# Attention feeding a rational feed-forward layer: q and k loaded as 512-byte rows, and their transposes done head by head as quarter-array products with the identity

## The chip, the cores and the metric

The kernel runs on one core of a Trainium2 chip. The time is device microseconds of that core. The kernel before took 615.79 us, the median of three runs (615.35 to 616.71); the execution that was profiled took 618.84 us.

## The reference, cut to what matters

Two stages follow each other: causal attention over 4 batches, 12 heads, 448 tokens and 64 numbers a head, and a feed-forward layer with a rational activation on the result, laid out as 1792 tokens by 768.

```python
# q, k, v: (4, 12, 448, 64) float32
scores = scale * np.matmul(q, k.transpose(0, 1, 3, 2))
scores = np.where(mask, -1000000000.0, scores)          # causal
scores = scores - np.max(scores, axis=-1, keepdims=True)
attn = np.exp(scores)
attn = attn / (np.sum(attn, axis=-1, keepdims=True) + 1e-09)
attn_out = np.matmul(attn, v)
x = attn_out.transpose(0, 2, 1, 3).reshape(1792, 768)
h = x @ w_in                                            # 768 -> 2048
P = a[0] + a[1] * h + a[2] * h**2 + a[3] * h**3
Q = 1.0 + abs(b[0]) * abs(h) + abs(b[1]) * h**2
out = (P / (Q + 1e-6)) @ w_out                          # 2048 -> 768
```

The weights come as 64-bit floats; the kernel turns them into 32-bit ones itself, beside the attention.

## The kernel before

Attention is done for 24 pairs of heads, one pair after the other in a loop over `p`. A pair fills the 128 rows of the matrix engine's array: head 0 in the lower 64, head 1 in the upper 64. The order of the work is written out by hand in the tables `HEAD`, `FIRST` and `ORDER`; every entry is a step and, behind an @, how many pairs it lags. All engines take the steps of one loop turn in the table's order. So in one turn the matrix engine (PE) does, in this order:

- `c` (line 365, tile psC): 32 transposes of the normalised exponentials of the pair before, each on a 64-row half of the array;
- `qk` (line 279, tile psA): the transposes of q and k of the *next* pair. The loaded tile holds 112 tokens on partitions, four blocks of tokens, both heads side by side, so one transpose takes 64 tokens (or the remaining 48) by 128 numbers, both heads at once. That is 2 tensors x 4 blocks x 2 (64 and 48 tokens, index `x`) = 16 transposes;
- `s` (line 311, tile psS): the scores of the pair, 7 query blocks of 64 rows against 64 to 448 keys, for each of the two heads. Every product sits on one quarter of the array: rows by head, columns by `half((1 + b + j) % 2)`. 14 products, which the trace shows as 28 matmuls, since a 32-bit product runs in two passes (a transpose runs in one);
- `d` (line 389, tile psD): exponentials times v of two pairs ago, 8 products on half the array's columns, 16 matmuls in the trace.

The other engines work beside it. VectorE (DVE) takes the masked maximum of each score block (line 322), copies half of psC (377) and converts weights (168, 174). ScalarE (ACT) does the exponentials with their sums (332), the other half of psC (375), the copy of psA into `QK` (294) and the results of psD (409). GpSimd (POOL) normalises the exponentials (346) and converts weights (158, 162). PSUM banks go round in two rings, so a matmul waits until ACT or DVE has read the bank's last content.

All transfers are issued by the SyncE queue (SP) in program order: q and k of the pair four turns ahead (line 247, four transfers of 112 KB), v of this pair (lines 253 and 256, three transfers), every second turn a 768 KB load of weights (143 or 148) and a 384 KB store (180). Every transfer waits for the landing of the one that stands eight places ahead of it, since eight completion semaphores are used in turn. v has three buffers, q and k four each. After the attention (about 145 us) the two matrix products of the feed-forward layer follow until the end.

Of the kernel before, what the change touches and what calls it, by code (L numbers as in the profile page):

```python
# [8 lines left out]
F32 = mybir.dt.float32  # L9
# [47 lines left out]
def kernel(  # L57
# [11 lines left out]
    nc = tc.nc  # L69
    B, H, S, D = q.shape  # L70
    DM, DFF = moe_w_in.shape
    P = 128
    CP = 112
    NB = S // CP
# [21 lines left out]
    ident = const.tile([P, P], F32, name="ident")  # L96
# [138 lines left out]
    raw, QK, AT, pv, SUM, REC, psa, pss, psr, psc, nmx = {}, {}, {}, {}, {}, {}, {}, {}, {}, {}, {}  # L235
# [3 lines left out]
    def stage_load(p):  # L239
        if p in raw:  # L240
            return
        b, hp = divmod(p, HP)
        raw[p] = {}
        for n, src in (("q", q), ("k", k)):
            t = raw[p][n] = ld.tile([CP, NB, 2, D], F32, tag=n, bufs=4, name=f"{n}raw")
            for j in range(2):
                nc.sync.dma_start(out=t[:, :, j], in_=src[b, 2 * hp + j].rearrange("(c p) d -> p c d", p=CP))

    def stage_load_v(p):
        b, hp = divmod(p, HP)  # L250
# [10 lines left out]
    def half(j):  # L261
        return slice(j * D, (j + 1) * D)
# [3 lines left out]
    def ring(x, name):  # L266
        if x:
            return ps_t.tile([P, 512], F32, tag="y", bufs=3, name=name)
        n = banks.pop(0)
        banks.append(n)  # L270
        return (ps_s if n == 3 else ps_t).tile([P, 512], F32, tag=f"x{n}", name=name)

    def qk_pe(p):
        ps = psa[p] = [ring(x, "psA") for x in range(2)]
        for n, src in enumerate(("q", "k")):
            for c in range(NB):
                for x, w in enumerate((QB, CP - QB)):
                    r, lo = slice(x * QB, x * QB + w), (n * NB + c) * w
                    nc.tensor.transpose(  # L279
                        ps[x][:, lo:lo + w], raw[p][src][r, c].rearrange("p j d -> p (j d)"), ident[r, r]  # L280
                    )
        if p == 0:
            keep_warm(4)

    def qk_ev(p, x):
        if p not in QK:
            QK[p] = qk.tile([P, 2, S], F32, tag="qk", name="qkt")
        lo, hi = x * QB, (QB, CP)[x]
        o = QK[p].rearrange("p n (c r) -> p (n c) r", r=CP)[:, :, lo:hi]
        i = psa[p][x][:, :2 * NB * (hi - lo)].rearrange("p (c r) -> p c r", r=hi - lo)  # L290
        if p < 2 and x == 1:
            nc.vector.tensor_copy(out=o, in_=i)
        else:
            nc.scalar.copy(out=o, in_=i)
# [132 lines left out]
    def conv(p, part):  # L427
# [17 lines left out]

    tasks = {
        "ld": stage_load, "lv": stage_load_v,
        "qk": qk_pe, "qx": lambda p: qk_ev(p, 0), "qy": lambda p: qk_ev(p, 1),
        "s": stage_b_pe, "m": stage_b_max, "e": stage_b_exp, "sm": stage_b_sum, "r": stage_b_rec, "n": stage_b_norm,
        "c": c_pe, "a": lambda p, h: c_ev(p, h, 0), "v": lambda p, h: c_ev(p, h, 1),  # L450
# [410 lines left out]
    with tc.manual_schedule():  # L861
# [13 lines left out]
        ld = es_r.enter_context(pool(name="ld", bufs=2, side="right"))  # L875
# [4 lines left out]
        for x in range(2):  # L880
            m = mask[half(x), S - QB:]
            nc.gpsimd.affine_select(
                out=m, in_=m, compare_op=ALU.is_ge, fill=-1e9 / SCALE, base=0, pattern=[[-1, QB]], channel_multiplier=1,
# [24 lines left out]
        def keep_warm(n):  # L908
            for _ in range(n):
                nc.tensor.matmul(idle, warm, warm, start=True, stop=True, skip_group_check=True)  # L910
# [89 lines left out]
        for j in range(HF):  # L1000
            n = j + 5
# [44 lines left out]
```

## Time and profile before

| what | us |
|---|---|
| median of three runs | 615.79 (615.35 to 616.71) |
| profiled execution | 618.84 |
| its span in the trace | 617.1 |
| PE busy in the span | 597.3 (97%) |
| DVE / ACT / POOL busy | 536.2 / 449.8 / 171.8 |

The span runs from the first to the last instruction of the program; 1.7 us of the profiled execution lie outside it. Busy time of PE counts a matmul from its start to its modelled end, and matmuls overlap in the pipeline, so the start times of successive groups tell more than the busy share. The trace is read by stage: the attention up to about 145 us, and the feed-forward layer after it. PE's granted clock is 1.00 (2.4 GHz) throughout.

### The profile page before, as it was taken

The numbers are of one execution on the slowest core, as the hardware profiler recorded it, in microseconds if no ns is written. First come the engines' busy times: TensorE is split into PE (matmuls) and PEld (weight loads), VectorE is DVE, ScalarE is ACT, GpSimd is POOL, SyncE is SP. The second block draws the span as 40 slices with busy tenths as digits, with TensorE's granted clock in tenths as the row PEclk, the third lists the DMA queues.
The fourth block names the chain that finished last, engine by engine and source line by source line (L and its number), as shares of the span: only waits on it lengthen the run. The fifth ranks groups of instructions, "written<-read, shape, count | busy, mean of one in ns | idle before, by whom it ended". The sixth has DMA issues, their size and how long they took to land.

```text
span 617.1 us, 12747 instructions
## 1 busy us (share of the span) xinstructions
PE 597.3 (97%) x4656; PEld 497.7 (81%) x4656; DVE 536.2 (87%) x1034; ACT 449.8 (73%) x920; POOL 171.8 (28%) x251
## 2 busy tenths in 40 slices
PE   7999999889999999999999999989999999999997
PEld 5666666557788888888888888878999999997886
DVE  4899999976689999999998888888999999986950
ACT  5999999986776867778877567566576776777721
POOL 3788888785544311112333100000000000000000
PEclk9999999999999999999999999999999999999999
DMA  8978697888468988889985663333263344148774
GB/s 163 239 176 213 171 217 206 204 201 276 145 264 286 332 311 304 304 304 313 353 303 197 216 240 106 141 128 129 102 216 122 126 153 149 57 157 319 236 237 177
DMA packets 105727, 131.00 MB, mean 212 GB/s; under 512 B 70592, under 2 KB 83008, under 8 KB 105664
## 3 DMA queue, kind: packets, MB, share of 16 engines
q1 hardware_dynamic: 105664, 130.18, 66.4%
q8 instruction: 37, 0.61, 0.4%
q14 instruction: 26, 0.21, 0.1%
HBM read 99.49 MB, written 30.67 MB: 211 GB/s over the span
## 4 chain that ended last, share of the span: by engine, by line
PE 69%; DVE 15%; ACT 7%; issue 4%; DMA 3%; POOL 2%; SPq 0%; ACTq 0%; DVEq 0%; POOLq 0%
PE psO L597 19%; PE psH L227 16%; PE psQ L699 12%; PE psM L593 10%; PE psD L389 4%; PE psS L311 4%; PE psC L365 3%; ACT e L332 2%; DVE psS L322 2%; DMA vraw<-in_v_dram 1%; DVE u L168 1%; PE psA L279 1%; DVE at L377 1%; POOL e L346 1%; DVE p L754 1%
## 5 line engine op out<-in xcount | busy, mean ns | idle before, releaser
L597 PE MATMUL psO<-whl,gh 128*128 128x512 f32 x448 | 160.0, 393 | 1.3 <-DMA whl<-whl 1.1
L227 PE MATMUL psH<-xs,whl 128*128 128x512 f32 x576 | 136.8, 391 | 0.5 <-DVE p L493 0.4
L593 PE MATMUL psM<-whl,gh 128*128 128x256 f32 x448 | 126.0, 282 | 0.0
L227 PEld LDWEIGHTS psH<-xs,whl 128*128 128x128 f32 x576 | 105.9, 188 | 22.6 <-DVE p L493 0.7
L597 PEld LDWEIGHTS psO<-whl,gh 128*128 128x128 f32 x448 | 84.0, 188 | 21.1 <-ACT kept L762 1.4
L346 POOL TENSOR_SCALAR e<-e,r 128x192 f32<-128x192 f32 (+6 forms) x168 | 80.0, 499 | 35.6 <-DVE r L342 18.6
L593 PEld LDWEIGHTS psM<-whl,gh 128*128 128x128 f32 x448 | 84.5, 189 | 1.3
L699 PE MATMUL psQ<-xpart,wq 128*128 128x384 f32 x432 | 78.5, 336 | 4.3 <-ACT xpart L615 1.7
L332 ACT ACTIVATE e<-psS,nm 128x448 f32<-128x448 f32 (+6 forms) x168 | 78.0, 506 | 6.0 <-DVE nm L322 5.7
L597 PE MATMUL psO<-whl,gl 128*128 128x512 f32 x224 | 81.2, 391 | 0.1
L699 PEld LDWEIGHTS psQ<-xpart,wq 128*128 128x128 f32 x432 | 74.8, 188 | 5.8 <-ACT xpart L615 2.0
L322 DVE CUSTOM_DVE_ANT_0 psS<-psS,mask 128x64 f32<-128x64 f32 (+6 forms) x168 | 65.3, 455 | 1.8 <-PE psS L311 1.7
L593 PE MATMUL psM<-whl,gl 128*128 128x256 f32 x224 | 63.1, 282 | 0.0
L389 PE MATMUL psD<-at,vraw 128*64 128x448 f32 (+3 forms) x384 | 47.6, 386 | 4.9 <-DMA vraw<-in_v_dram 2.5
L500 ACT ACTIVATE w<-w 128x512 f32<-128x512 f32 x32 | 20.2, 632 | 42.0 <-DVE w L485 42.0
L158 POOL TENSOR_SCALAR u<-raw 128x768 f32<-128x768 f32 x32 | 35.3, 1103 | 55.0 <-DMA raw<-in_moe_w_out_dram 23.4
L389 PEld LDWEIGHTS psD<-at,vraw 128*64 128x64 f32 x384 | 27.0, 136 | 29.0 <-issue 12.0
L597 PEld LDWEIGHTS psO<-whl,gl 128*128 128x128 f32 x224 | 42.0, 188 | 9.3 <-DVE gl L790 0.4
L311 PE MATMUL psS<-qkt 64*64 64x192 f32 (+6 forms) x672 | 48.1, 391 | 1.2 <-ACT e L332 0.9
L593 PEld LDWEIGHTS psM<-whl,gl 128*128 128x128 f32 x224 | 42.3, 189 | 0.0
L377 DVE COPY at<-psC 128x512 f32<-128x512 f32 x48 | 32.5, 680 | 8.6 <-PE psC L365 8.5
L332 ACT ACTIVATION_READ_ACCUMULATOR e<-psS,nm 128x1 f32 x168 | 39.6, 237 | 0.0
(110 smaller groups left out, 1101.9 us busy)
## 6 DMA issues: line engine op xcount, KB each, us to landing
whl<-whl SPq DMA_DIRECT2D x64, 768.0 KB, 4.4
w<-w SPq DMA_DIRECT2D x54, 384.0 KB, 5.0
raw<-in_moe_w_in_dram SPq DMA_DIRECT2D x16, 768.0 KB, 5.7
raw<-in_moe_w_out_dram SPq DMA_DIRECT2D x16, 768.0 KB, 5.6
w<-u SPq DMA_DIRECT2D x29, 384.0 KB, 3.1
qraw<-in_q_dram SPq DMA_DIRECT2D x48, 112.0 KB, 3.6
kraw<-in_k_dram SPq DMA_DIRECT2D x48, 112.0 KB, 3.6
out_dram<-osb SPq DMA_DIRECT2D x13, 384.0 KB, 3.3
```

The lines of the kernel that those rows point to most:

```text
L158: nc.gpsimd.tensor_scalar(out=u.bitcast(F32), in0=y, scalar1=0.0, scalar2=1.0, op0=ALU.mult, op1=ALU.mult)
L227: nc.tensor.matmul(ps, w[:, c * P:(c + 1) * P], xs[ck, part, c // K3][:, c % K3], start=(c == 0 and n == 0), stop=(c == KD - 1 and n == 2),)
L311: nc.tensor.matmul(pss[p, b][half((1 + b + j) % 2)], QK[p][half(j), 0, b * QB:(b + 1) * QB], QK[p][half(j), 1, :b_w[b]], start=True, stop= ...
L322: nc.vector.tensor_tensor_reduce(out=s, in0=s, in1=mask[:, S - w:], scale=-SCALE, scalar=3e38, op0=ALU.add, op1=ALU.min, accum_out=nmx[p][ ...
L332: nc.scalar.activation(out=E[p % 2][i][:, :w], in_=pss[p, i], func=AF.Exp, bias=nmx[p][:, i:i + 1], scale=-1.0, accum_out=SUM[p % 2][:, i, ...
L346: nc.gpsimd.tensor_scalar(out=e, in0=e, scalar1=REC[p][:, i:i + 1], scalar2=0.0, op0=ALU.mult, op1=ALU.add)
L377: nc.vector.tensor_copy(out=o, in_=i)
L389: nc.tensor.matmul(ps[half(j), lo * QB:S], v[:, j, c], a[h][:, slot * QB:(slot + 7 - lo) * QB], start=(c == 0), stop=(c == 3), skip_group_ ...
L500: nc.scalar.activation(out=w, in_=w, func=AF.Abs)
L593: nc.tensor.matmul(acc["m", k], g, w[:, 512:], start=first and (k % 2 == 0 or each), stop=last, skip_group_check=True)
L597: nc.tensor.matmul(acc[k], g, w[:, :512], start=first, stop=last)
L699: nc.tensor.matmul(q_bank[j, bank], w[:, wp_, c * P:(c + 1) * P], xp_[:, c], start=(first and n == 0), stop=(n == 3 * K3 - 1), skip_group_ ...
```

## The change

One pair's q is now one transfer, and its k another, instead of two each. A partition `p` gets, of each half `g` of a head's tokens, the two neighbouring tokens 2p and 2p+1, which lie next to each other in memory: runs of 512 bytes in place of 256. The tile holds the heads as an outer index, so the two heads of a token are no longer side by side, and one transpose can't take both. Each is done by itself, as an ordinary 32-bit product with the identity, on the quarter of the array given by `x` (rows) and the head `j` (columns). The copy out of PSUM puts the tokens back in order with a step of two in its writes.

```diff
-            t = raw[p][n] = ld.tile([CP, NB, 2, D], F32, tag=n, bufs=4, name=f"{n}raw")
-            for j in range(2):
-                nc.sync.dma_start(out=t[:, :, j], in_=src[b, 2 * hp + j].rearrange("(c p) d -> p c d", p=CP))
+            t = raw[p][n] = ld.tile([CP, 2, 2, 2, D], F32, tag=n, bufs=4, name=f"{n}raw")
+            nc.sync.dma_start(
+                out=t.rearrange("p j g c d -> p (j g) (c d)"),
+                in_=src[b, 2 * hp:2 * hp + 2].rearrange("j (g p c) d -> p (j g) (c d)", g=2, c=2),
+            )
...
-                    nc.tensor.transpose(
-                        ps[x][:, lo:lo + w], raw[p][src][r, c].rearrange("p j d -> p (j d)"), ident[r, r]
-                    )
+                    for j in range(2):
+                        nc.tensor.matmul(
+                            ps[x][half(j), lo:lo + w], raw[p][src][r, j, c // 2, c % 2], ident[r, r],
+                            start=True, stop=True, skip_group_check=True,
+                        )
...
-        o = QK[p].rearrange("p n (c r) -> p (n c) r", r=CP)[:, :, lo:hi]
-        i = psa[p][x][:, :2 * NB * (hi - lo)].rearrange("p (c r) -> p c r", r=hi - lo)
+        o = QK[p].rearrange("p n (g r c) -> p (n g) c r", g=2, c=2)[:, :, :, lo:hi]
+        i = psa[p][x][:, :2 * NB * (hi - lo)].rearrange("p (g c r) -> p g c r", c=2, r=hi - lo)
```

On PE, one turn of the loop stood like this around the transposes (psA's two tiles are its two banks, for 64 and 48 tokens; a size is rows out by columns moved):

```order
L365 MATMUL psC_954<-ident_69,e06_184 128x64
L279 MATMUL psA_979<-ident_69,qraw_601 128x64 [waits DMAHW6_49,DMAHW5_49,Activation_49]
L279 MATMUL psA_980<-ident_69,qraw_601 128x48 [waits PE_49]
...
L279 MATMUL psA_979<-ident_69,kraw_604 128x64 [waits DMAHW7_49,DMAHW0_49]
L279 MATMUL psA_980<-ident_69,kraw_604 128x48
...
L311 MATMUL psS_1008<-qkt_885 64x320 [waits Activation_49]
```

With the change the same place reads (one row is one product, x2 two alike; lines moved by three or four):

```order
L369 MATMUL psC_1338<-ident_69,e06_184 128x64
L282 MATMUL psA_1363<-ident_69,qraw_957 64x64 [waits DMAHW1_49,Activation_49]
L282 MATMUL psA_1363<-ident_69,qraw_957 64x64
L282 MATMUL psA_1364<-ident_69,qraw_957 64x48 [waits PE_49]
...
L282 MATMUL psA_1363<-ident_69,kraw_959 64x64 [waits DMAHW2_49]
L282 MATMUL psA_1364<-ident_69,kraw_959 64x48 x2
...
L315 MATMUL psS_1406<-qkt_1271 64x320 [waits Activation_49]
```

Nothing moved past anything: between psC and psS stand 32 products of 64 output rows in place of 16 transposes of 128, and q and k each wait for one transfer instead of two.

On SP, the transfers of one turn that loads weights (raw) were:

```order
L247 DMA qraw<-in_q_dram 112x4x64 [waits DMAHW3_49]
L247 DMA qraw<-in_q_dram 112x4x64 [waits DMAHW4_49]
L247 DMA kraw<-in_k_dram 112x4x64 [waits DMAHW5_49]
L247 DMA kraw<-in_k_dram 112x4x64 [waits DMAHW6_49]
L148 DMA raw_869<-in_moe_w_out_dram 128x1536 [waits DMAHW7_49,DVE_49]
L253 DMA vraw_175<-in_v_dram 128x3x64 [waits DMAHW0_49,PE_49]
L253 DMA vraw_175<-in_v_dram 128x3x64 [waits DMAHW1_49,PE_49]
L256 DMA vraw_175<-in_v_dram 64x2x64 [waits DMAHW2_49,PE_49]
```

and are now:

```order
L246 DMA qraw<-in_q_dram 112x4x128 [waits DMAHW1_49]
L246 DMA kraw<-in_k_dram 112x4x128 [waits DMAHW2_49]
L148 DMA raw_961<-in_moe_w_out_dram 128x1536 [waits DMAHW3_49,DVE_49]
L255 DMA vraw_175<-in_v_dram 128x3x64 [waits DMAHW4_49,PE_49]
L255 DMA vraw_175<-in_v_dram 128x3x64 [waits DMAHW5_49,PE_49]
L258 DMA vraw_175<-in_v_dram 64x2x64 [waits DMAHW6_49,PE_49]
```

Two transfers fewer stand ahead of the weights and of v, and eight semaphores now span more bytes. ACT, DVE and POOL keep their instructions and their order.

## Rows read from the trace of the kernel before

**Rows 1.** Busy time by stage; columns: stretch, length, each engine's busy time, PEclk, DMA.

```profile
0.00:21.00 21.00, 17.12 (x220) 12.14 (x220) 11.49 (x53) 14.30 (x48) 8.83 (x34) 1.00 0.89 189
21.00:37.30 16.30, 16.30 (x280) 11.29 (x276) 15.52 (x58) 16.26 (x57) 13.41 (x24) 1.00 0.84 203
37.30:94.00 56.70, 56.45 (x924) 37.59 (x920) 56.70 (x209) 55.49 (x199) 47.99 (x81) 1.00 0.82 202
94.00:145.30 51.30, 45.85 (x756) 31.57 (x752) 44.48 (x164) 44.86 (x161) 39.86 (x66) 1.00 0.83 217
145.30:617.00 471.70, 461.57 (x2488) 405.06 (x2488) 408.02 (x553) 318.90 (x463) 61.70 (x49) 1.00 0.62 214
```

**Rows 2.** Timeline of PE, one undisturbed turn; columns: start us, us, engine, line, what.

```profile
21.00 1.21 PE L365 MATMUL psC<-ident,e 64*128 64x64 f32 x32
22.05 0.41 PE L279 MATMUL psA<-ident,qraw 64*128 64x64 f32 x8
...
22.64 1.95 PE L311 MATMUL psS<-qkt 64*64 64x320 f32 x28
24.52 1.95 PE L389 MATMUL psD<-at,vraw 128*64 128x448 f32 x16
26.40 0.28 PE L365 MATMUL psC<-ident,e 64*128 64x64 f32 x2
```

**Rows 3.** Busy time of line 279 alone, by stage; x is its matmuls, 16 a pair.

```profile
0.00:16.50 16.50, 2.43 (x48) 1.99 (x48) 1.00 0.84 162
16.50:37.30 20.80, 2.69 (x64) 2.33 (x64) 1.00 0.90 221
37.30:94.00 56.70, 7.08 (x160) 5.76 (x160) 1.00 0.82 202
94.00:143.60 49.60, 4.92 (x112) 4.19 (x112) 1.00 0.82 211
```

**Rows 4.** Timeline of weight loads (PEld) in the scores of one pair, late in psS.

```profile
63.59 0.14 PEld L311 LDWEIGHTS psS<-qkt 64*64 64x64 f32 x2 [0.28 <-ACT at L375]
63.91 0.26 PEld L311 LDWEIGHTS psS<-qkt 64*64 64x64 f32 x10 [0.18 <-issue]
```

**Rows 5.** Timeline of PE in the last stage; in brackets the idle time before.

```profile
110.56 2.14 PE L389 MATMUL psD<-at,vraw 128*64 128x448 f32 x16 [1.21 <-DVE nm L322]
...
122.85 2.27 PE L389 MATMUL psD<-at,vraw 128*64 128x448 f32 x16 [1.19 <-DVE nm L322]
...
136.56 2.27 PE L389 MATMUL psD<-at,vraw 128*64 128x448 f32 x16 [2.52 <-DMA vraw<-in_v_dram]
138.75 0.28 PE L365 MATMUL psC<-ident,e 64*128 64x64 f32 x2
...
143.65 1.53 PE L365 MATMUL psC<-ident,e 64*128 64x64 f32 x32
```

**Rows 6.** Timeline of SP (time to issue), then landings of single transfers issued at 126.88, 128.00.

```profile
124.59 1.12 SPq L247 DMA_DIRECT2D qraw<-in_q_dram  x2
...
126.88 0.44 SPq L143 DMA_DIRECT2D raw<-in_moe_w_in_dram  x1
128.00 1.32 SPq L253 DMA_DIRECT2D vraw<-in_v_dram  x2
...
raw<-in_moe_w_in_dram SPq DMA_DIRECT2D x1, 768.0 KB, 8.4
...
vraw<-in_v_dram SPq DMA_DIRECT2D x1, 96.0 KB, 8.5
```

**Rows 7.** DMA packets, MB, share of 16 engines: 2 to 9 us, 105.4 to 106 us.

```profile
q1 hardware_dynamic: 5544, 1.37, 98.8%
...
q1 hardware_dynamic: 155, 0.16, 83.8%
```

**Rows 8.** Groups of ACT instructions by line; count, busy us, mean ns.

```profile
L202 ACT CAST whl<-w 128x768 fp32r<-128x768 f32 x18 | 15.1, 843 | 2.3 <-DMA w<-w 2.3
L166 ACT ACTIVATE raw<-raw 128x768 f32<-128x768 f32 x12 | 10.8, 909 | 0.0
```

## The prediction

> **What bounds the kernel now.** I read first the busy time by stage [rows 1]. After 145.3 us the matrix engine (PE) is busy 461.57 of 471.70 us, and no instruction the change touches runs there: the question is the 145 us of attention. There the stages differ. From 21 to 37.3 us PE is busy all the time and VectorE is not; from 37.3 to 94 VectorE is busy for 56.70 of 56.70 us; from 94 on PE lacks 5.45 of 51.3 us and nobody is full.
>
> Then the timeline of one undisturbed turn [rows 2]. Its steps start at 21.00 (psC), 22.05 (psA), 22.64 (psS), 24.52 (psD) and 26.40 (next psC): a turn of 5.40 us with no idle time in it. This is PE's own price of a pair, of which the transposes of q and k take 22.64 - 22.05 = 0.59 us. The last turn has no such transposes (138.75 to 143.65, 4.90 us [rows 5]).
>
> With 5.40 us as PE's price, the lost time can be counted by stage; the count of pairs comes from line 279 alone, 16 matmuls each [rows 3]: 3 pairs before 16.5 us, 4 up to 37.3, 10 up to 94, 7 after. The ten turns of the middle stage take 56.7 us, 5.67 each, which is VectorE's pace, not PE's. The last stage has seven turns with transposes and one without, 7 x 5.40 + 4.90 = 42.7 us of PE work, and takes 49.6: 6.9 us are lost. Three products with v (psD) start late, after 1.21, 1.19 and 2.52 us of idle time, and are then longer than the undisturbed 1.95 (2.14, 2.27, 2.27 [rows 2, 5]): 5.75 us of the 6.9. The profile names VectorE for two of these and the transfer of v for the third. I put all three down to v: the last was issued at 128.00 and took 8.5 us, to 136.5, right before the start at 136.56 [rows 5, 6].
>
> **The change, part by part.** *Products in place of transposes (adds PE time).* Per pair 16 transposes become 32 products of two passes, 64 matmuls. In psS and psD such 32-bit products already run on parts of the array. psD works on two column halves, each with 448 + 320 + 192 + 64 = 1024 columns in two passes, 2048, in 26.40 - 24.52 = 1.88 us: 0.92 ns a column. psS uses all four quarters; the fullest has the even blocks, 64 + 192 + 320 + 448 = 1024 columns, again 2048 with both passes, and again 1.88 us [rows 2]. So four quarters run beside each other at the price of one. The new psA gives each of the two quarters with 64 tokens 8 products x 2 passes x 64 = 1024 columns: 0.94 us at that price, 0.35 more than 0.59. That scales all of the group. But psC's 32 transposes take 1.05 us and psA's 16 take 0.59, which is 0.029 us each and 0.13 fixed; with 0.13 fixed in psD too, a column costs 0.854 ns, and the new psA 0.87 + 0.13 = 1.00 us, 0.41 more. The upper bound is 0.48: today psA follows psC on the same array halves and psS follows on quarters; with the change it is the other way round, and if half of the fixed 0.13 us came in ahead of psA and none went behind it, that is 0.07 on top. I take +0.40 us a pair, next to the reading with the fixed part, so a turn of 5.80.
>
> Enough matmuls must also be issued: 64 with their weight loads in 0.94 us, 15 ns each. Late in psS ten loads follow in a row within 0.26 us, of which the last one itself lasts 0.14 [rows 4]: 13 ns each. That just holds.
>
> *The copy out of PSUM (line 294).* Same two ACT instructions a pair, writes now in steps of two. ACT already has an operation that reads and writes in steps of two: 909 ns for 768 columns at line 166, against 843 for the plain cast at line 202 [rows 8]. 66 ns on 768 is at most 0.08 us on the 896 columns of a pair; ACT, busy 55.49 us in ten turns of the middle stage [rows 1], then stays near 5.55 + 0.08 a turn, below PE's 5.80, so I take nothing. On VectorE it happens twice in the first 11 us.
>
> *Transfers (removes SP and DMA time).* Per pair SP issues two transfers fewer at 0.56 us each (1.12 for two [rows 6]), 1.1 us. The packets become half as many and twice as long. 5544 packets of 256 bytes took 98.8% of 16 engines for 7 us: 20 ns each; 155 of 1024 bytes took 83.8% for 0.6 us: 52 ns [rows 7]. 512 bytes then cost between 20 ns (as the small ones) and 40 (twice, nothing gained); on the line between the two rows 31, which I take, as the longer packets clearly have a fixed share. A pair has 1792 packets of 256 bytes, 2.24 us of all engines; 896 packets cost 1.1 to 2.2, at 31 ns 1.7 us: half a microsecond less a pair.
>
> The Trainium skill, "DMA: Bandwidth & Descriptors", section Specifications, says that line rate needs at least 512 bytes and that less is read, modified and written. No row shows a packet of 512 bytes; those of 1024 (20 GB/s) do run better than those of 256 (13 GB/s). By its 27 GiB/s an engine 512 bytes would take about 18 ns (an estimate), less than the 20 ns measured for 256, the pair would save 1.2 us, and every wait for v would go: the sum below would fall by 0.6 us.
>
> *What this does to v.* v stands behind q, k and the weights on SP and on the DMA engines. It lands earlier by the 1.1 us of issue and by 0.5 us of transfer, and it is wanted 0.4 us later. 2.0 us earlier removes waits of 1.2 and 1.2 and leaves about 0.6 of the third; the stretched psD groups shrink to 1.95, since their later transfers come earlier too.
>
> *Start.* The first psA isn't held up by k any more, but ends no earlier than now; +0.1 us. The next two pairs lie in a stretch in which PE is busy 17.12 of 21.00 us [rows 1], ahead of its steady turns. I take them as covered; if that cover is gone, they cost 0.8 us.
>
> **Sum, by stage.** Before 16.5 us: +0.1. To 37.3, PE is the bound: 4 x 0.40 = +1.6. To 94, PE takes over from VectorE: 10 x 5.80 = 58.0, plus 0.3 for turns in which VectorE needs longer than that, against 56.7: +1.6. After 94: 7 x 5.80 + 4.90 = 45.5, plus 0.6 of v's wait and 0.7 for the smaller losses that remain (1.15 us are there today), 46.8 against 49.6: -2.8. Together +0.5 us: PE pays 8.4 us for its products, and gets nearly all of it back from slack and from waits for v. From the profiled execution's 618.84 us that makes 619.3; its distance to the median (3.05) taken as it is, 616.3.
>
> **The rivals.**
>
> *Nothing is left of the waits (faster).* At 0.35 us a pair and with no residue anywhere: 4 x 0.35 = 1.4, 57.5 - 56.7 = 0.8, and 45.15 - 49.6 = -4.45, together -2.2: 613.6; with 0.40 and no residue -1.1. For it: turns without waits stand in rows, and 5.80 us is above the pace of the other engines. Against it: turns in the last stage lose 1.15 us that have nothing to do with v. At 0.35 it is faster by over 0.2% while under 1 us of residue stays.
>
> *v goes on waiting (slower).* v still stands behind 768 KB of weights, whose load took 8.4 us from issue [rows 6], and q and k may gain nothing if a 512-byte packet costs 40 ns, or if the runs aren't joined. Then the 5.75 us stay: 45.5 + 5.75 + 0.7 = 51.95 against 49.6, +2.3, and with the other stages' +3.3 it is +5.6: 621.4. It ends on the slower side from 1.3 us of v's wait on. Against it: SP's queue and the semaphores get freer whatever a packet costs.
>
> *PE can't issue them (slower).* The rate of 13 ns holds for ten loads. The only long row of small matmuls is psC: 32 in 1.05 us, 33 ns each [rows 2]. If that is the pace of issue, 64 take 2.1 us, a pair 1.5 us more, a turn 6.9: 4 x 1.5 = 6, 69 - 56.7 = 12.3 and 53.2 - 49.6 = 3.6, together +22: 638. The Trainium skill, "TensorE: Matmul & The Clock Gate" (section on 56 against 53.3 ns), gives a floor of 25 ns from start to start for small matmuls; were it one for the whole array and not for one part, 64 would take 1.6 us, which makes +11 and 627. The ten loads at 13 ns speak against both, and psC's 33 ns fits two halves of 64 columns at 0.92 ns as well.
>
> **How the numbers follow.** A measurement of this kernel can tell about 0.2% (1.2 us) from no change: under 614.6 is faster, over 617.0 slower. My forecast has 0.55: of it 0.05 falls below 614.6, 0.40 within, 0.10 above. Nothing left of the waits 0.17, v goes on waiting 0.16, PE can't issue 0.12. So faster 0.22, same 0.40, slower 0.38. The range goes from 613.6 to 622.0 and leaves out the issue rival and little else.
>
> **What would show it.** Right: psA 0.9 to 1.05 us from its start to psS's in an undisturbed turn, turns of 5.75 to 5.88 almost everywhere, no idle time over 0.7 us before psD after 94 us, 512-byte packets (43,008 fewer under 512 bytes), the first matmul of the feed-forward layer at about 145.8 us instead of 145.3. Wrong: a psA of 1.6 us or more (issue), idle time before psD as today (v), or turns over 5.9 with a full ACT (the copy). The forecast fails most easily at 0.40: each 0.05 us there is 1 us in all.

## The result

The changed kernel took 626.2 us, the median of five runs (623.31 to 626.87), the kernel before 615.79 (615.35 to 616.71): with a recorded ratio of 1.0133, 95% interval 1.0097 to 1.0168 (the quotient of the two medians is 1.0169). It is slower by over 0.2%; the forecast was 616.3 us with a range to 622.0. The profiled execution took 623.33 us with a span of 621.5.

The profile after, first its engines and its DMA queues (lines of the page; x is a number of instructions, and the queue lines give packets, MB and a share of 16 engines):

```profile
PE 605.6 (97%) x5808; PEld 509.0 (82%) x5808; DVE 539.8 (87%) x1034; ACT 452.8 (73%) x920; POOL 168.3 (27%) x251
...
DMA packets 83464, 131.14 MB, mean 211 GB/s; under 512 B 26816, under 2 KB 60736, under 8 KB 83392
...
q1 hardware_dynamic: 83392, 130.18, 65.2%
q8 instruction: 46, 0.75, 0.5%
```

The same lines of the page of before:

```profile
PE 597.3 (97%) x4656; PEld 497.7 (81%) x4656; DVE 536.2 (87%) x1034; ACT 449.8 (73%) x920; POOL 171.8 (28%) x251
...
DMA packets 105727, 131.00 MB, mean 212 GB/s; under 512 B 70592, under 2 KB 83008, under 8 KB 105664
...
q1 hardware_dynamic: 105664, 130.18, 66.4%
q8 instruction: 37, 0.61, 0.4%
```

PE got 1152 matmuls and 1152 weight loads more, 48 and 48 a pair. The queue q8, of the kind "instruction", brought 9 packets more, each of 16 KB (a second queue of this kind, q14, has 26 packets in both kernels). 2304 more PE instructions in 9 more packets is one packet for every 256 instructions.

An undisturbed turn of after, which answers to [rows 2] (timeline of PE):

```profile
29.62 1.21 PE L369 MATMUL psC<-ident,e 64*128 64x64 f32 x32
30.76 0.68 PE L282 MATMUL psA<-ident,qraw 64*64 64x64 f32 x32
31.28 0.63 PE L282 MATMUL psA<-ident,kraw 64*64 64x64 f32 x32
31.75 1.91 PE L315 MATMUL psS<-qkt 64*64 64x320 f32 x28
33.58 1.95 PE L393 MATMUL psD<-at,vraw 128*64 128x448 f32 x16
35.46 1.20 PE L369 MATMUL psC<-ident,e 64*128 64x64 f32 x32
```

psA takes 31.75 - 30.76 = 0.99 us and the turn 35.46 - 29.62 = 5.84, against 0.59 and 5.40 before [rows 2].

The other stretches are compared between steps that every kernel has: the start of the first psD, of the fourth, of the fourteenth, the first matmul of the feed-forward layer, and the end. Windows of after (columns as in [rows 1]):

```profile
21.72:39.42 17.70, 17.70 (x422) 12.32 (x421) 16.41 (x60) 17.14 (x59) 11.33 (x21) 1.00 0.76 194
39.42:98.08 58.66, 58.66 (x1403) 41.48 (x1401) 57.80 (x209) 56.89 (x199) 46.45 (x81) 1.00 0.78 202
98.08:147.02 48.94, 47.03 (x1058) 32.85 (x1056) 44.72 (x160) 43.89 (x152) 35.78 (x64) 1.00 0.74 202
150.40:621.50 471.10, 462.64 (x2488) 406.58 (x2488) 408.25 (x553) 318.90 (x463) 63.48 (x49) 1.00 0.61 214
```

The first three stretches in the profile of before:

```profile
19.12:35.43 16.31, 16.31 (x278) 11.30 (x277) 15.39 (x58) 16.27 (x58) 13.42 (x24) 1.00 0.96 227
35.43:92.16 56.73, 56.48 (x924) 37.59 (x921) 56.73 (x209) 55.53 (x197) 48.02 (x81) 1.00 0.79 191
92.16:141.76 49.60, 44.39 (x722) 30.43 (x720) 43.35 (x162) 43.38 (x152) 39.07 (x65) 1.00 0.81 212
```

The feed-forward layer takes 471.1 us, as before [rows 1]. The whole difference arises in the attention: the first psD starts 2.6 us later (21.72 against 19.12), the next two stretches are 1.39 and 1.93 us longer, and the last one is only 0.66 shorter. psD no longer waits for v anywhere. What stands in its place is seen in the list of PE's waits of after (engine, line, what it waited for: us in total, times, longest):

```profile
PE psA L282 <- issue: 3.4, 3, 2.0
PE psQ L703 <- ACT xpart L619: 1.7, 1, 1.7
PE psS L315 <- issue: 1.3, 1, 1.3
...
```

"issue" is idle time for which the profile shows nothing that PE waited for. Its three long places, in the timeline of PE:

```profile
12.57 0.50 PE L282 MATMUL psA<-ident,kraw 64*64 64x64 f32 x19 [2.00 <-issue]
...
19.50 0.49 PE L282 MATMUL psA<-ident,kraw 48*64 48x48 f32 x18 [1.24 <-issue]
...
113.76 1.47 PE L315 MATMUL psS<-qkt 64*64 64x320 f32 x12
116.58 1.08 PE L315 MATMUL psS<-qkt 64*64 64x384 f32 x16 [1.35 <-issue]
```

They lie in the middle of a group, between two like products. Counted from the start, 449, 705 and 5313 instructions of PE (matmuls, weight loads and waits for semaphores; called records from here on) stand ahead of them in the trace: 256 apart, and then 18 x 256. At each of them a packet of the queue "instruction" has just come in and ends 1.4 us before PE goes on (packets at 10.02 to 11.20, 17.03 to 18.12 and 114.19 to 115.23). One of the three, in the DMA view of after from 114.1 to 115.3 us:

```profile
DMA packets 82, 0.46 MB, mean 380 GB/s; under 512 B 5, under 2 KB 5, under 8 KB 81
## 3 DMA queue, kind: packets, MB, share of 16 engines
q1 hardware_dynamic: 81, 0.44, 91.6%
q8 instruction: 1, 0.02, 5.4%
```

So the theory that the experiments test is this: **PE waits for its own code.** The code comes in blocks of 256 PE instructions, in one packet each. A block lasts as long as PE needs for 256 instructions: before, 924 + 921 records in 56.73 us, 7.9 us a block; after, 1403 + 1401 in 58.66, 5.4 us. With the borders of the blocks counted from the stops, the packet of a block starts, in the attention, between 1.7 us ahead of and 5.5 us behind the moment at which PE enters the block before it, over all profiles of both kernels; then it takes about 1 us, and PE another 1.4. A block that lasts 7.9 us hides all of that, one of 5.4 us does not when the packet is late by over 3 us.

### The profile page after: what moved, and what is told of

Same layout as the page of the kernel before. It is cut to its first block, busy times and chain, and to the rows that moved or that the text cites. A ratio compares the mean times of both kernels' runs of the same rounds, so it can differ in the third digit from the quotient of the medians.

```text
span 621.5 us, 14974 instructions
## 1 busy us (share of the span) xinstructions
PE 605.6 (97%) x5808; PEld 509.0 (82%) x5808; DVE 539.8 (87%) x1034; ACT 452.8 (73%) x920; POOL 168.3 (27%) x251
## 5 line engine op out<-in xcount | busy, mean ns | idle before, releaser
L350 POOL TENSOR_SCALAR e<-e,r 128x192 f32<-128x192 f32 (+6 forms) x168 | 77.4, 483 | 45.9 <-DVE r L346 23.1
L703 PE MATMUL psQ<-xpart,wq 128*128 128x384 f32 x432 | 79.9, 340 | 2.9 <-ACT xpart L619 1.7
L703 PEld LDWEIGHTS psQ<-xpart,wq 128*128 128x128 f32 x432 | 76.3, 191 | 4.3 <-ACT xpart L619 2.0
L158 POOL TENSOR_SCALAR u<-raw 128x768 f32<-128x768 f32 x32 | 38.1, 1189 | 54.9 <-DMA raw<-in_moe_w_in_dram 24.4
L393 PEld LDWEIGHTS psD<-at,vraw 128*64 128x64 f32 x384 | 25.4, 136 | 24.6 <-issue 13.1
L168 DVE SCALAR_TENSOR_TENSOR u<-raw,u 128x768 uint32<-128x768 uint32 x32 | 40.7, 1270 | 0.0
L315 PEld LDWEIGHTS psS<-qkt 64*64 64x64 f32 x672 | 26.5, 133 | 14.7 <-issue 8.0
```

The costliest lines, as they stand in the source:

```text
L158: nc.gpsimd.tensor_scalar(out=u.bitcast(F32), in0=y, scalar1=0.0, scalar2=1.0, op0=ALU.mult, op1=ALU.mult)
L168: nc.vector.scalar_tensor_tensor(out=c_u[m], in0=raw[:, :, 0], scalar=29, in1=c_u[m], op0=ALU.logical_shift_right, op1=ALU.bitwise_or,)
L315: nc.tensor.matmul(pss[p, b][half((1 + b + j) % 2)], QK[p][half(j), 0, b * QB:(b + 1) * QB], QK[p][half(j), 1, :b_w[b]], start=True, stop= ...
L350: nc.gpsimd.tensor_scalar(out=e, in0=e, scalar1=REC[p][:, i:i + 1], scalar2=0.0, op0=ALU.mult, op1=ALU.add)
L393: nc.tensor.matmul(ps[half(j), lo * QB:S], v[:, j, c], a[h][:, slot * QB:(slot + 7 - lo) * QB], start=(c == 0), stop=(c == 3), skip_group_ ...
L703: nc.tensor.matmul(q_bank[j, bank], w[:, wp_, c * P:(c + 1) * P], xp_[:, c], start=(first and n == 0), stop=(n == 3 * K3 - 1), skip_group_ ...
```

## The experiments

**The two halves of the change, each alone.** First the transfers:

```diff
-            t = raw[p][n] = ld.tile([CP, NB, 2, D], F32, tag=n, bufs=4, name=f"{n}raw")
+            t = raw[p][n] = ld.tile([CP, 2, 2, 2, D], F32, tag=n, bufs=4, name=f"{n}raw")
...
-                        ps[x][:, lo:lo + w], raw[p][src][r, c].rearrange("p j d -> p (j d)"), ident[r, r]
+                        ps[x][:, lo:lo + w], raw[p][src][r, c // 2, c % 2].rearrange("p c d -> p (c d)"), ident[r, r]
```

> The new transfers (one for q, one for k, 512-byte rows) with the old number of PE instructions: 16 transposes of 128 columns a pair, which take two neighbouring tokens of one head where the kernel before takes one token of both heads, so q and k reach the scores mixed up; all else is the kernel before. Theory A (PE waits for its own code: the queue 'instruction' brings PE 16-KB blocks, one for every 256 PE instructions, and with the change a block is used up in 5.3 us in place of 7 to 8): 37 blocks as before, none of them late, no idle time of PE put down to issue over 0.4 us, v no longer waited for, the feed-forward layer begins about 4 to 5 us earlier than 145.3, time 610.5 to 612.5. Theory B (the fuller transfers themselves hold PE up, since eight outstanding transfers are now twice as many bytes): the waits of 2.00 and 1.24 us at the start and of 1.35 us at 115 us are there as in the changed kernel, time about 615 to 617.

Measured: 615.59 us (613.07 to 616.63) against 616.64 of before in the same job, ratio 0.9971 (0.9949 to 0.9994). 37 packets of code, no idle time put down to issue, none for v. Theory B fell: the transfers hold nobody up. But theory A's number fell too: the gain is 0.3% and not 0.7. Windows of this kernel, for the second and third of the stretches above:

```profile
37.71:94.24 56.53, 56.30 (x925) 37.04 (x921) 56.53 (x209) 55.40 (x198) 47.83 (x82) 1.00 0.78 205
94.24:139.03 44.79, 43.79 (x723) 28.86 (x721) 43.23 (x162) 42.97 (x152) 38.95 (x65) 1.00 0.82 223
```

The last stretch did shrink by 4.8 us against the first profile of before, yet the time fell by only 1. That led to the question of how typical that profile is (below).

Then the products, with the transfers of before:

```diff
-                    nc.tensor.transpose(
-                        ps[x][:, lo:lo + w], raw[p][src][r, c].rearrange("p j d -> p (j d)"), ident[r, r]
-                    )
+                    for j in range(2):
+                        nc.tensor.matmul(
+                            ps[x][half(j), lo:lo + w], raw[p][src][r, c, j], ident[r, r],
+                            start=True, stop=True, skip_group_check=True,
+                        )
```

> The new products (32 a pair, 64 matmuls) with the old transfers (two each for q and k, 256-byte rows). Theory A: 46 blocks of code for all engines in place of 37, blocks of PE used up in 5.3 us, and one to four of them late by 0.5 to 2.5 us, each at a PE record that lies a multiple of 256 behind the first such stop; turns of 5.83 us; waits for v 0 to 3 us; time 621 to 628, as the changed kernel's. Theory B: no idle time of PE put down to issue over 0.4 us, and 616 to 619 from the longer turns alone (+0.44 us a pair where PE is the bound).

Measured: 624.38 us (622.81 to 627.89), ratio 1.0121 (1.0064 to 1.0179), 46 packets of code. Waits of PE of this kernel from the first psD on:

```profile
PE psS L313 <- issue: 3.4, 2, 2.0
PE psA L280 <- issue: 1.8, 2, 1.4
PE psC L367 <- issue: 1.4, 1, 1.4
...
```

The stops are there again, now in psC too, and again at records that are a multiple of 256 away from the 449th. So the products bring the loss, stops and all, with either kind of transfer; waits for v are gone with them alone, too.

**Fewer instructions for the same work of the array.** A transpose shows as one matmul in the trace, a product as two. Head 1, whose rows begin at 64, gets a 128-column transpose here, which brings it into the upper half, with something useless in the lower; head 0's 64-column transpose is then written over that:

```diff
-                    for j in range(2):
-                        nc.tensor.matmul(
-                            ps[x][half(j), lo:lo + w], raw[p][src][r, j, c // 2, c % 2], ident[r, r],
-                            start=True, stop=True, skip_group_check=True,
-                        )
+                    t = raw[p][src].rearrange("p j g c d -> p (j g c d)")
+                    nc.tensor.transpose(ps[x][:, lo:lo + w], t[r, (NB + c - 1) * D:(NB + c + 1) * D], ident[r, r])
+                    nc.tensor.transpose(ps[x][:D, lo:lo + w], t[r, c * D:(c + 1) * D], ident[r, r])
```

> The changed kernel with the same transfers and the same columns on the array, but half the new instructions: for each block of tokens one transpose of 128 columns, whose upper half is head 1 (its lower half is overwritten), and one of 64 columns for head 0. Both run in one pass, so the fullest quarter of the array gets 2 x 8 x 64 = 1024 columns as with the products (2 passes x 8 x 64). 32 matmuls and 32 loads a pair in place of 64 and 64: a turn has 216 PE records in place of 280, and a block of 256 lasts about 6.9 us of a turn of 5.8. Theory A (late code is most of the loss): 40 blocks, stops behind late blocks under 1.5 us in all, 617 to 620 us. Rival (the array time of the products is the loss, the stops only moved it): 623 to 627 us, turns as before.

Measured: 622.16 us (619.74 to 622.99, ten runs), ratio 1.0077 (1.0052 to 1.0103). 40 packets of code; waits of PE from the first psD to 160 us:

```profile
PE psC L367 <- POOL e L348: 0.6, 2, 0.4
PE psH L227 <- ACT e L334: 0.2, 1, 0.2
```

There is no stop left in that stretch. Turns are as long as with the products: from the second psD to the third, 33.65 - 27.81 = 5.84 us in this kernel's timeline. A block of code lasts longer, as the windows of this kernel show for the second and third stretch (2162 records in 59.28 us, 7.0 us a block):

```profile
39.56:98.84 59.28, 59.28 (x1082) 41.46 (x1080) 58.85 (x209) 56.52 (x199) 45.78 (x81) 1.00 0.75 196
98.84:145.79 46.95, 46.34 (x834) 31.98 (x832) 44.78 (x160) 43.45 (x152) 36.47 (x64) 1.00 0.75 210
```

The time lies between the two expectations, 2.2 us over theory A's end and 0.8 under the rival's: both are half right. By the medians, the stops account for about 4 us of the changed kernel's 10 (626.2 and 626.7 against 622.2), and what stays, 5 us over before, goes with the longer turns: array time.

**How typical the profiles are.** Both kernels were profiled again, unchanged.

> The changed kernel once more, for its two levels (623.3 and 626.3 us). Theory A: the queue wait of a block differs from run to run, so the stops on PE put down to issue sum up to about 4.6 us in a run of 623.3 and to about 7.5 us in one of 626.3, or else the 3 us lie elsewhere in the program (the profile will show where); the stops stand at PE records a multiple of 256 from each other.

> The kernel before once more, for a second profile, since the first was of an execution of 618.84 us, 3 us over the median. Theory A2 (part of the waits for v of the first profile were of that one execution): 615 to 616.5 us, and the waits of psD for v after 94 us sum up to about 2 us in place of 5. Rival: the same waits (about 5 us), and what is shorter lies elsewhere. By both, no idle time of PE put down to issue over 0.4 us.

> The kernel before, a third profile. Its runs lie between 613.6 and 620.7 us. Theory A2: executions over 617 us are those in which psD waits for v after 94 us (2 us or more in all, as in the first profile), executions under 616.5 us have none of it (as in the second). Rival: the waits for v have nothing to do with it, and an execution over 617 us has its time elsewhere.

> The kernel before, a fourth profile, with the same expectation: waits of psD for v of 2 us or more where the execution takes over 617 us, none where it takes under 616.5 us.

> The changed kernel, a third profile. Theory A: the time follows the stops of PE behind late blocks of code: with transposes twice (620.4 us of span, 0.4 us of stops) as the base, 4 us of stops stand for a span of 621 to 622.5, 7 to 8 us for one of 624 to 626. Rival: the span doesn't follow the stops.

Measured, with the other kernels' profiles. "Attention" runs from the first psD to the first matmul of the feed-forward layer; the waits are PE's idle time in that stretch, by the lists of waits:

| profile | execution, us | first psD | attention | waits there, us |
|---|---|---|---|---|
| before, third | 614.62 | 18.88 | 122.1 | v 1.2 |
| before, again | 615.73 | 21.23 | 121.2 | none for v |
| before, fourth | 617.53 | 20.92 | 122.9 | v 1.8 |
| before, the one shown ahead | 618.84 | 19.12 | 126.2 | v 4.9 |
| transfers alone | 615.76 | 21.42 | 121.2 | none for v |
| transposes twice | 622.16 | 21.97 | 127.3 | none to issue |
| changed | 623.33 | 21.72 | 128.7 | issue 1.5 |
| changed, again | 626.46 | 22.03 | 130.9 | issue 3.0 |
| changed, third | 629.73 | 21.70 | 134.3 | issue 3.5, and half clock for 3.4 us |
| products alone | 627.89 | 20.48 | 134.1 | issue 6.6 |

The rows of before follow one line: attention takes 121.2 us plus its waits for v (of psD, of which some are put down to the last VectorE instruction, as in [rows 5]). Theory A2 holds, but for its bounds: the third profile had 1.2 us of such waits in an execution of 614.62 us, the fourth 1.8 at 617.53, and the second none where about 2 were expected. The first profile, on which the prediction rests, was the one with by far the most. The column of the first psD has something else in it: in the second and the fourth profile of before, with the transfers alone and with the transposes twice, PE's clock stood at half for 3.4 us ahead of it, from between 16.5 and 17.6 us on. In the changed kernel it did not, and the first psD is late by the stops.

Windows of the second profile of before:

```profile
37.51:94.04 56.53, 56.31 (x925) 37.36 (x921) 56.53 (x209) 55.37 (x197) 47.80 (x82) 1.00 0.83 203
94.04:138.88 44.84, 43.79 (x723) 28.92 (x721) 43.31 (x162) 42.93 (x152) 39.00 (x65) 1.00 0.88 231
```

Its last stretch takes 44.84 us, without any help, against 49.60 in the first profile: it is the same as with the new transfers alone (44.79). Three of the four profiles of before held little or nothing for the transfers to win (waits of 0, 1.2 and 1.8 us).

In the changed kernel the long stop of the last stretch is at the same product in all three profiles, behind 5313 records. In the second, from PE's timeline:

```profile
116.22 1.47 PE L315 MATMUL psS<-qkt 64*64 64x320 f32 x12
119.10 1.08 PE L315 MATMUL psS<-qkt 64*64 64x384 f32 x16 [1.41 <-issue]
```

And in the third:

```profile
117.11 1.47 PE L315 MATMUL psS<-qkt 64*64 64x320 f32 x12
120.54 1.41 PE L315 MATMUL psS<-qkt 64*64 64x384 f32 x16 [1.96 <-issue]
121.88 3.26 PE L393 MATMUL psD<-at,vraw 128*64 128x448 f32 x16
```

The packet of that block came at 116.90 and at 118.26, 5.0 and 5.5 us after PE had entered the block before. The time follows the stops in order but not in size: the idle time counts from the modelled end of the last matmul (116.22 + 1.47, to 119.10, is 1.41), while from start to start 1.95 us pass there, and the third profile also lost time to a low clock.

**The place of a stop.**

```diff
-        keep_warm(8)
+        keep_warm(3)
+        for _ in range(21):
+            nc.tensor.matmul(idle[:, :4], warm, warm[:, :4], start=True, stop=True, skip_group_check=True)
```

> The changed kernel with 64 PE records more ahead of the first product (5 of the 8 idle warm-up matmuls are replaced by 21 with 4 columns, in a stretch in which PE waits for the first q anyway). Theory A: what is late is a block of code, so the stops stay at the same PE records (449 and 705 from the start, and every further one at a multiple of 256 from there), and stand 64 records earlier in the program: the first among the transposes of q of the third pair and not of k, the second among those of q of the fourth pair. Theory B: they stay at the same products (k of the third pair, k of the fourth), now 513 and 769 records from the start. Time 622 to 628 by both.

Measured: 631.34 us (630.21 to 631.95), ratio 1.0224 (1.0175 to 1.0273). The small matmuls took 8.96 us, far more than PE waits there for the first q; the first products began at 11.44 instead of 4.73, and the packets of the first two blocks ended 5.1 and 4.8 us ahead of their use: neither stop of the start occurred, at the old or the new place, so the question as it was put got no answer. Two stops of over 0.5 us remained (0.66 and 0.85 us between starts), 7 and 15 blocks of 256 records behind the 449th. That bears theory A out: with 64 records more ahead of it, a stop that stayed with its product would stand 64 records off these places.

**As many instructions, no array work.**

```diff
                 start=(c == 0), stop=(c == 3), skip_group_check=True,
             )
+            for _ in range(12):
+                nc.tensor.nop("pad")
```

> The kernel before with 12 empty instructions for PE behind each of the 8 products of psD, 96 a pair: as many more PE instructions as the change brings (64 matmuls and 64 loads in place of 16 and 16), and no work for the array. Theory A (late code): 46 blocks of code in place of 37; blocks used up in 5.3 to 5.5 us; between two and eight stops of PE of 0.5 to 2.5 us behind late blocks; 619 to 626 us. Rival (the array's or the sequencer's own time for many small matmuls): no stops, and 615 to 618 us; if an empty instruction has a price of its own, psD is longer in each turn by the same amount, without stops.

Measured: 725.37 us (723.53 to 726.34), ratio 1.1737. An empty instruction has a price of its own, far over what was expected: ten turns took 104.8 us, where the second profile of before has 56.5. In psD, PE now stops for "issue" behind each product, as its timeline shows:

```profile
22.61 0.51 PE L389 MATMUL psD<-at,vraw 128*64 128x192 f32 x2 [0.21 <-issue]
23.54 0.51 PE L389 MATMUL psD<-at,vraw 128*64 128x192 f32 x2 [0.42 <-issue]
24.41 0.30 PE L389 MATMUL psD<-at,vraw 128*64 128x64 f32 x2 [0.36 <-issue]
```

As a test of late code it says one thing: 46 packets, as in the changed kernel, and none late, the nearest 4.9 us ahead of its use, where a block lasts 9 to 11 us. So the number of blocks alone doesn't make them late. Whether the slower pace keeps them in time or the emptier DMA engines (a share of 0.46 in these ten turns, against 0.78 in the changed kernel) isn't told apart here; the run with transposes twice, with a share of 0.75 and blocks of 7.0 us, speaks for the pace.

**The change for the last pairs alone.** The three places of the change under a condition, with LATE = 16:

```diff
+            if p >= LATE:
+                t = raw[p][n] = ld.tile([CP, 2, 2, 2, D], F32, tag=n, bufs=4, name=f"{n}raw")
...
+                    if p >= LATE:
+                        for j in range(2):
+                            nc.tensor.matmul(
...
+        if p >= LATE:
+            o = QK[p].rearrange("p n (g r c) -> p (n g) c r", g=2, c=2)[:, :, :, lo:hi]
```

> The change for the pairs 16 to 23 alone (whose products stand in the turns after about 85 us, where PE waited for v), the kernel before for the pairs 0 to 15. Theory A: no late block ahead of 85 us, 40 blocks in all; behind it turns of 5.83 us without waits for v, but one to two late blocks of 1 to 2 us; 614.5 to 618 us. If code is never late there, 612.5 to 614.5, which would beat both kernels.

Measured: 621.69 us (617.89 to 623.83 in nine of ten runs, 627.35 in one), ratio 1.006 (1.003 to 1.009). The median lies above both expected ranges. 40 packets; in the profile, of an execution of 618.99 us, among its shortest, attention takes 124.6 us with one late block, 0.72 us of idle time at 112 us. That much is what theory A has, at its lower end. Why the other executions took up to 5 us more isn't known, since only this one was profiled. The kernel is faster than the changed one (626.2) and slower than the one before.

**Products for one head, transposes for the other.**

```diff
-                    for j in range(2):
-                        nc.tensor.matmul(
-                            ps[x][half(j), lo:lo + w], raw[p][src][r, j, c // 2, c % 2], ident[r, r],
-                            start=True, stop=True, skip_group_check=True,
-                        )
+                    nc.tensor.transpose(ps[x][:D, lo:lo + w], raw[p][src][r, 0, c // 2, c % 2], ident[r, r])
+                    nc.tensor.matmul(
+                        ps[x][half(1), lo:lo + w], raw[p][src][r, 1, c // 2, c % 2], ident[r, r],
+                        start=True, stop=True, skip_group_check=True,
+                    )
```

> A step between: the products of head 1 stay, those of head 0 become transposes of one pass, on their own quarters of the array. 248 PE records a turn in place of 280; the array's fullest quarter (head 1, 64 tokens) keeps its 1024 columns, so turns of 5.83 us. A block of 256 lasts 6.0 us in place of 5.3. Theory A: 43 blocks, stops of 1 to 4 us in all in place of 4.6 to 7.6, 619.5 to 624 us, between the changed kernel and the run with transposes twice. Rival (array time): 623 to 627 us.

Measured: 818.38 us (817.82 to 819.55), ratio 1.326. Both theories missed it, and as a step between it says nothing. A piece of psA in PE's timeline:

```profile
42.83 0.24 PE L281 MATMUL psA<-ident,qraw 64*64 64x64 f32 x1
43.01 0.33 PE L282 MATMUL psA<-ident,qraw 64*64 64x64 f32 x2
43.26 0.23 PE L281 MATMUL psA<-ident,qraw 48*64 48x48 f32 x1
43.42 0.31 PE L282 MATMUL psA<-ident,qraw 48*64 48x48 f32 x2
```

A transpose, a product and the next transpose start 0.18 and 0.25 us apart, at a granted clock of 1.00 (2.4 GHz), where 64 matmuls of products alone take 0.99 us. The two kinds hardly run beside each other here.

## Why the prediction was wrong

*The products' price was right.* psA takes 0.99 us to the start of psS (1.00 forecast), a turn 5.84 (5.80, upper bound 5.88). Four quarters do run beside each other, and the pace of issue, which was a rival at 627 and 638, holds: 64 matmuls in 0.99 us are 15 ns each. The 25 ns that the Trainium skill gives as a floor ("TensorE: Matmul & The Clock Gate", section on 56 against 53.3 ns) are none for the whole array here. The rival's 627 is near the result by chance; its mechanism isn't there.

*The copy out of PSUM* costs nothing, as forecast: the copy's mean is 609 ns after and 606 before, by the groups of ACT.

*The packets.* 43,776 fewer under 512 bytes (43,008 forecast). Their price was mis-sized. In the packet records of the two traces, the 21,504 packets of 512 bytes took 33.9 ns in the mean, not 31, and the 256-byte ones of before 19.0, not 20. The 18 ns that followed from the Trainium skill ("DMA: Bandwidth & Descriptors", Specifications: line rate from 512 bytes on) were about half of what was measured. A pair saves (1792 x 19.0 - 896 x 33.9) / 16, 0.2 us of the engines, and not 0.5. The difference had no effect, since v came in time anyway.

*The waits for v*, the first failed step. In "After 94" the sum took 2.8 us back. 5.75 us of waits were read from one execution and carried over to the median by "its distance to the median (3.05) taken as it is". But the distance was those waits: without them the attention takes 121.2 us, with them 126.2 (of these 5.0 us the second profile, at the median, gives 2.1 back by its later first psD). Both can't be had, the low median and the gain from waits that the median doesn't contain. Against the second profile of before, the last stretch with transposes twice is 46.95 - 44.84 = 2.1 us longer, not 2.8 shorter: 4.9 us of the miss. The middle stretch adds 59.28 - 56.53 = 2.75 in place of 1.6. Of the 1.15 us more, 0.4 are ten turns of 5.84 in place of 5.80, 0.2 the base of 56.53 in place of 56.7, and the rest turns of 5.9 to 6.1 us, for which 0.3 in all was set aside; VectorE is busy for 58.85 of those 59.28 us, but what lengthens these turns wasn't tested. The first comes to 17.59 - 16.28 = 1.3 for three turns, as forecast. In all, 127.3 - 121.2 = 6.1 us is what the array's time costs the attention.

*Code that comes late*, the second failed step: the sum has no term for it. PE's instructions were counted for their pace of issue, not for where they come from. On top of the 127.3 us, the three profiles of the changed kernel have 1.4, 3.6 and 7.0 us (the last with a stretch at half clock). At the start, where +0.1 was forecast with the next two pairs "covered", two stops of 2.00 and 1.24 us fall into the third and fourth pairs, and the first psD comes 2.6 us later than in the first profile of before. Against that one execution the change costs 623.33 - 618.84 = 4.5 us where +0.5 was forecast; the three long stops are 4.6. So against its own profile the sum failed by the code nearly alone, and on the way from there to the median by the waits for v. Between the two medians the account is 4.9 us for those waits, 1.1 for the middle stretch and about 4 for the code, against a miss of 9.9.

That late code causes the stops was shown from four sides: they stand at multiples of 256 records, they come with the products and not with the transfers, they go when the same array time is bought with fewer instructions, and they follow the packets one by one. For the last, take the start times of PE's records and the ends of the packets in the attention of all profiles but those of the runs with empty instructions and with one head transposed: 243 borders of blocks in twelve profiles. PE never crossed a border less than 1.1 us after the end of its packet. At 21 borders over 0.5 us passed from start to start, and at each of these the packet had ended 1.1 to 1.6 us before PE went on; where it had ended earlier, no more than 0.4 us passed.

Why a packet starts late stays open. That it waits behind other transfers was only argued, from busy engines at the time, and no run changed that alone. The trace doesn't settle it either: from 112.40 to 114.15 us, right before the packet at 114.19 started, the other transfers took 52.2% of the engines and no more.

*The rivals.* "v goes on waiting" gave the right sign and half of the size (5.6 us of 10.4), with the wrong cause: no wait for v is left. The signs that were named (psA, turns, packets, no idle time over 0.7 us ahead of psD) came true in the first profile but for two: idle time appeared elsewhere, and the feed-forward layer began at 150.4 instead of 145.8. In the second profile a stop of 1.0 us does stand in a psD, behind its first 12 matmuls, for code and not for v.

## What to carry to other kernels

Before counting a wait as something to win, look whether a second profile has it: a profile 0.5% over the median had waits that the median hadn't, and a gain from them can't be taken off the median too. Count the instructions of the busiest engine per microsecond as a resource of its own: here code in blocks of 256 that last 7 us or more in the mean never stopped the engine for over 0.4 us; in blocks of 5.4 us it did so three to five times in each profile of the changed kernel. Where the same array time can be had with fewer instructions, that is worth more than the array's busy time shows (4 us here).

## What the runs showed of the hardware that was not expected

- PE's code came in 16-KB packets of a queue of its own, one for every 256 instructions (9 more for 2304), and PE went on 1.1 to 1.6 us after the end of a packet that was late (21 stops).
- 512-byte packets took 33.9 ns in the mean, 256-byte ones 19.0: the longer rows bought little.
- An empty instruction on PE cost about 50 ns: (104.8 - 56.5) / 960, an upper figure, since the mean clock there was 0.89 of full.
- Transposes and products that alternate on different quarters started 0.16 to 0.25 us apart at full clock; products by themselves 15 ns, the transposes of psC 33 [rows 2].
- PE's granted clock fell from 2.4 to 1.2 GHz for 3.4 us in some executions. In the third profile of the changed kernel it did so right after the stop at 118 us (psD took 3.26 us there instead of 1.95). In the second and the fourth profile of before, with the transfers alone and with the transposes twice, it did so between 16.5 and 17.6 us, behind waits of PE for ACT and POOL between 11 and 17 us. The first and the third profile of before have such waits too, and no fall. In six profiles it also fell once in the feed-forward layer, at 411 to 421 us. What decides it stays open.

```profile
121.20:124.50 3.30, 3.30 (x18) 1.36 (x13) 2.77 (x11) 2.28 (x10) 0.79 (x1) 0.50 0.29 74
...
16.50:19.80 3.30, 3.30 (x48) 2.69 (x48) 1.70 (x5) 2.28 (x6) 1.30 (x3) 0.50 1.12 307
...
16.50:19.80 3.30, 3.30 (x54) 1.83 (x50) 3.08 (x15) 3.02 (x9) 2.02 (x5) 1.00 1.11 306
```

These are windows of the third profile of the changed kernel and of the fourth and the third of before; 0.50 and 1.00 are the granted clock.
